# Attention and mixer on one core: rebuilt with 32-row score tiles, transposes on VectorE, packed last chunks and a list-scheduled order

## The chip, the cores and the metric

The kernel runs on 1 core of one Trainium2 chip. The metric is the device time of one execution in microseconds, given as the median of 3 runs. A core has TensorE (PE in the profile; its weight loads are PEld), VectorE (DVE), ScalarE (ACT), GpSimd (POOL) and SyncE (SP). Each engine works off its own instructions in order; DMAs are issued from the queues of POOL, SP and ACT.

## The reference

Block-wise causal attention (blocks of 64 positions), then a mixer over tokens and over channels, with both results added to what went in:

```python
B, H, S, D = 8, 8, 576, 64
scores = q @ k.T / sqrt(D)                    # per batch and head: 576 x 576
scores = where(pos_i // 64 >= pos_j // 64, scores, -1e9)
attn = softmax(scores)
x = (attn @ v) of all heads side by side      # 576 x 512 per batch
u = x + (relu(x.T @ w_tok1) @ w_tok2).T       # token mix, inner size 256
out = u + relu(u @ w_ch1) @ w_ch2             # channel mix, inner size 1536
```

All inputs and the output are fp32 in device memory; the kernel computes in bf16 with fp32 accumulation.

## The kernel before

576 rows are four chunks of 128 and a last one of 64, which is treated as a full chunk padded with zeros. The work of a batch is four `attention_pair` calls (two heads each) and one mixer.

`load_qk_pair` (lines 109 to 126) loads q and k of two heads by POOL's queue, which casts fp32 to bf16 on the way, two DMAs a head and tensor (512 rows at line 116, 64 rows at line 122). `attention_pair` (line 181) transposes q and k on PE against the identity (lines 186 and 192, five 128x128 tiles each), copies the results out of PSUM (DVE at lines 188 and 194, ACT at line 195), and so has the head dimension on the partitions: 64 rows for each of two heads. The k of one head keeps the other head's 64 rows at zero (`kTa`, `kTb`), so that a product of 128 rows gives one head's scores. Scores (line 214) are kept as keys on the partitions and queries on the columns; the table `REGIONS` cuts the causal half into six products of 512, 64, 448, 320, 192 and 64 columns, 1,600 in all. ACT takes the exponential (lines 223 to 226), DVE writes zeros into the four half blocks that the mask excludes (lines 230 to 233), and the product with v (line 238) is taken in 15 products of 65 columns, the 65th a column of ones that gives the sum. DVE takes the reciprocal (line 247) and multiplies (lines 248 and 254) into `x_sb`.

`token_mix` (line 261) is 10 products of 512 columns for `aT` (line 266) and 10 for `u_sb` (line 283), where DVE adds x (line 290). `transpose_u` turns u in 20 tiles (line 301). `channel_gT` (line 314) computes the inner layer for 576 rows as two halves of 288 columns, 12 x 2 x 4 = 96 products (line 319), each half rectified on ACT or DVE (line 326). `channel_h2_out` (line 330) takes 12 products of 512 columns for each of five chunks (line 336), DVE adds u (line 343), and SP's queue writes the batch out in two DMAs (lines 346 and 350).

The main loop (line 352) puts the mixer of the batch before between the four attention pairs of a batch. The framework sets the order on each engine from that program order. Rings of buffers limit how far ahead it runs: four raw q and k buffers, three sets of exponentials, three PSUM banks each for `sc` and `mps`, two for transposes. The first two pairs' q and k are loaded before anything else; the channel weights are issued behind the attention of batch 0 (line 385).

Of the kernel before, what the change touches and what calls it, by code (L numbers as in the profile page):

```python
# [10 lines left out]
BF16 = mybir.dt.bfloat16  # L12
EXP = mybir.ActivationFunctionType.Exp
# [5 lines left out]
class Ring:  # L19

    def __init__(self, pool, n, shape, dtype, name):
        self.tiles = [
            pool.tile(shape, dtype, name=f"{name}{i}", uniquify=False)
            for i in range(n)
        ]
        self.i = 0

    def next(self):
        t = self.tiles[self.i % len(self.tiles)]
        self.i += 1  # L30
        return t
# [3 lines left out]
def kernel(  # L35
# [11 lines left out]
    nc = tc.nc  # L47
# [5 lines left out]
    NS = (S + 127) // 128  # L53
    SCH = [min(128, S - 128 * i) for i in range(NS)]
    SP = 128 * NS
    NDM = DM // 128
    NDT = DT // 128
    NDC = DC // 128
    scale = 1.0 / math.sqrt(D)

    consts = ctx.enter_context(tc.tile_pool(name="consts", bufs=1))
    wpool = ctx.enter_context(tc.tile_pool(name="wpool", bufs=1))
    ring_p = ctx.enter_context(tc.tile_pool(name="ring_p", bufs=1))
    qkT_p = ctx.enter_context(tc.tile_pool(name="qkT", bufs=4))
    mix_p = ctx.enter_context(tc.tile_pool(name="mix_p", bufs=2))
    out_p = ctx.enter_context(tc.tile_pool(name="out_p", bufs=2))
    small_p = ctx.enter_context(tc.tile_pool(name="small_p", bufs=4))

    ps_at = ctx.enter_context(tc.tile_pool(name="ps_at", bufs=3, space=bass.MemoryType.PSUM))
    ps_tr = ctx.enter_context(tc.tile_pool(name="ps_tr", bufs=2, space=bass.MemoryType.PSUM))  # L70
    ps_mm = ctx.enter_context(tc.tile_pool(name="ps_mm", bufs=3, space=bass.MemoryType.PSUM))

    r_qraw = Ring(ring_p, 4, [128, NS, 2, D], BF16, "qraw")
    r_kraw = Ring(ring_p, 4, [128, NS, 2, D], BF16, "kraw")
    r_kta = Ring(ring_p, 4, [128, SP], BF16, "kTa")
    r_ktb = Ring(ring_p, 4, [128, SP], BF16, "kTb")
    r_v1 = Ring(ring_p, 6, [128, NS, 66], BF16, "v1")
    r_e0 = Ring(ring_p, 3, [128, 512], BF16, "e0")
    r_e1 = Ring(ring_p, 3, [128, 576], BF16, "e1")
    r_e2 = Ring(ring_p, 3, [128, 576], BF16, "e2")  # L80
    r_e3 = Ring(ring_p, 3, [128, 128], BF16, "e3")
    r_x = Ring(ring_p, 3, [128, NS, DM], BF16, "x_sb")
    r_u = Ring(ring_p, 2, [128, NS, DM], BF16, "u_sb")
    r_gt = Ring(ring_p, 2, [128, NDC, SP], BF16, "gT")

    def init_pads():
        for t in r_qraw.tiles + r_kraw.tiles:
            nc.vector.memset(t[64:128, 4], 0.0)
        for t in r_kta.tiles:
            nc.scalar.memzero(t[64:128, :])  # L90
        for t in r_ktb.tiles:
            nc.scalar.memzero(t[0:64, :])
        for t in r_v1.tiles:
            nc.scalar.memzero(t[64:128, 4, :])
            nc.vector.memset(t[:, 0:4, 64:65], 1.0)
            nc.vector.memset(t[0:64, 4, 64:65], 1.0)
        for t in r_e1.tiles + r_e2.tiles:
            nc.scalar.memzero(t[:, 512:576])
        for t in r_e3.tiles:
            nc.scalar.memzero(t)  # L100
        for t in r_x.tiles + r_u.tiles:
            nc.scalar.memzero(t[64:128, 4, :])
        for t in r_gt.tiles:
            nc.scalar.memzero(t[:, :, S:SP])

    ident = consts.tile([128, 128], BF16)
    make_identity(nc, ident)

    def load_qk_pair(b, hp, split=1):
        tiles = []  # L110
        for src, ring in ((q, r_qraw), (k, r_kraw)):
            t = ring.next()
            for hh in range(2):
                for f in range(split):
                    c0, c1 = 4 * f // split, 4 * (f + 1) // split
                    nc.gpsimd.dma_start(  # L116
                        out=t[:, c0:c1, hh, :],
                        in_=src[
                            b, 2 * hp + hh, 128 * c0 : 128 * c1, :
                        ].rearrange("(c p) d -> p c d", p=128),  # L120
                    )
                nc.gpsimd.dma_start(  # L122
                    out=t[0:64, 4, hh, :], in_=src[b, 2 * hp + hh, 512:576, :]
                )
            tiles.append(t)
        return tiles

    first_pair = load_qk_pair(0, 0)
    second_pair = load_qk_pair(0, 1)
    init_pads()  # L130

    w1_sb = wpool.tile([128, NS, DT], BF16)
    nc.gpsimd.dma_start(
        out=w1_sb[:, 0:4, :],
        in_=moe_w_tok1[0:512, :].rearrange("(c p) t -> p c t", p=128),
    )
    nc.gpsimd.dma_start(out=w1_sb[0:64, 4, :], in_=moe_w_tok1[512:576, :])
    nc.vector.memset(w1_sb[64:128, 4, :], 0.0)

    w2_sb = wpool.tile([128, NDT, SP], BF16)  # L140
    nc.gpsimd.dma_start(
        out=w2_sb[:, :, 0:S], in_=moe_w_tok2.rearrange("(c p) s -> p c s", p=128)
    )
    nc.vector.memset(w2_sb[:, :, S:SP], 0.0)

    wc1_sb = wpool.tile([128, NDM, DC], BF16)
    wc2_sb = wpool.tile([128, NDC, DM], BF16)

    def load_channel_weights():
        for c in range(NDM):  # L150
            nc.gpsimd.dma_start(
                out=wc1_sb[:, c, :], in_=moe_w_ch1[128 * c : 128 * (c + 1), :]
            )
        for c in range(0, NDC, 2):
            nc.gpsimd.dma_start(
                out=wc2_sb[:, c : c + 2, :],
                in_=moe_w_ch2[128 * c : 128 * (c + 2), :].rearrange(
                    "(c p) t -> p c t", p=128
                ),
            )  # L160

    REGIONS = {
        0: (0, 0, 0, 512),
        5: (1, 0, 512, 64),
        1: (1, 64, 128, 448),
        2: (2, 0, 256, 320),
        3: (2, 320, 384, 192),
        4: (3, 330, 512, 64),
    }

    def exp_lhsT(e, I, J):
        if J == 4:
            return e[3][:, 0:128]
        i0 = 128 * I
        if J == 0 and I == 4:
            J = 5
        tix, c0, ist, wdt = REGIONS[J]
        col = c0 + (i0 - ist)
        return e[tix][:, col : col + 128]

    def attention_pair(b, hp, x_sb, preloaded=None):
        qraw, kraw = preloaded if preloaded is not None else load_qk_pair(b, hp)

        qT_ps = ps_tr.tile([128, SP], BF16, name="trp")
        for c in range(NS):
            nc.tensor.transpose(qT_ps[:, 128 * c : 128 * (c + 1)], qraw[:, c], ident)
        qT = qkT_p.tile([128, SP], BF16, name="qT")
        nc.vector.tensor_copy(qT, qT_ps)  # L188

        kT_ps = ps_tr.tile([128, SP], BF16, name="trp")  # L190
        for c in range(NS):
            nc.tensor.transpose(kT_ps[:, 128 * c : 128 * (c + 1)], kraw[:, c], ident)  # L192
        kTh = [r_kta.next(), r_ktb.next()]
        nc.vector.tensor_copy(kTh[0][0:64, :], kT_ps[0:64, :])  # L194
        nc.scalar.copy(kTh[1][64:128, :], kT_ps[64:128, :])  # L195

        for hh in range(2):
            h = 2 * hp + hh
            kT = kTh[hh]

            v1 = r_v1.next()
            nc.gpsimd.dma_start(  # L202
                out=v1[:, 0:4, 0:64],
                in_=v[b, h, 0:512, :].rearrange("(c p) d -> p c d", p=128),
            )
            nc.gpsimd.dma_start(out=v1[0:64, 4, 0:64], in_=v[b, h, 512:576, :])  # L206

            sc_pool, sc_name = (
                (ps_mm, "mps") if (b == 0 and hh == 0) else (ps_at, "sc")
            )  # L210
            sc = [sc_pool.tile([128, 512], FP32, name=sc_name) for _ in range(4)]
            for J, (tix, c0, ist, wdt) in REGIONS.items():
                j0 = 128 * (J if J != 5 else 0)
                nc.tensor.matmul(  # L214
                    out=sc[tix][:, c0 : c0 + wdt],
                    lhsT=kT[:, j0 : j0 + 128],
                    rhs=qT[:, ist : ist + wdt],
                    start=True,
                    stop=True,
                )  # L220

            e = [r_e0.next(), r_e1.next(), r_e2.next(), r_e3.next()]
            nc.scalar.activation(e[0], sc[0], EXP, scale=scale)  # L223
# [129 lines left out]
    for b in range(B + 1):  # L353
# [15 lines left out]
        if prev is not None:  # L369
            channel_gT(p_uT, p_gT, 4, 8)  # L370
# [48 lines left out]
```

## Time and profile before

| | us |
|---|---|
| median of 3 runs | 414.12 (414.06 to 414.85) |
| span of the profiled execution | 412.9 |
| the profiled execution's time outside the span, from the median | 1.2 |
| SP's output DMA of 1 MB, issue to landing (median) | 4.3 |
| channel weight DMA of 256 KB, issue to landing (median) | 11.9 |
| HBM read / written | 35.78 MB / 9.44 MB |

The span runs from the first to the last instruction on the chip. The profile has, for each engine, the busy time and the count of its instructions; groups of instructions by line, with the mean time of one and the idle time ahead of them with what ended it; the order of time; and DMA queues with their packets. The ends of matmuls are modelled: a product's row shows its whole passage through the array, and many overlap, so the rate is read from start to start in a long run of equal products. The granted clock is given for each stretch, 1.00 being full.

### The profile page before, as it was taken

Reading aid. Unit: us, or ns where it says so; the run is one execution under the profiler, and the core shown is the slowest. Engines: PE = TensorE matmul, PEld = TensorE weight load, DVE = VectorE, ACT = ScalarE, POOL = GpSimd, SP = SyncE. Lnnn points to the kernel's source line nnn. Section 1 sums busy time; section 2 is a strip of 40 time slices with the busy share of each in tenths; the row PEclk is TensorE's granted clock in tenths of the full one; section 3 lists DMA queues with packets and bytes.
Section 4 is the critical chain, followed back from the end, with each engine's and each line's share of the span. In section 5 each row is a group of like instructions: output and inputs, shape, how many; then the busy total and the mean of one; then the engine's idle time right before and its main releaser. Section 6 shows DMA issues by size and latency. Waiting matters only on the chain.

```text
span 412.9 us, 8622 instructions
## 1 busy us (share of the span) xinstructions
PE 368.6 (89%) x3194; PEld 229.3 (56%) x3232; DVE 175.8 (43%) x674; ACT 221.4 (54%) x507; POOL 261.0 (63%) x403
## 2 busy tenths in 40 slices
PE   1676659999999999999999999999999999999996
PEld 1454247754676456744666457744666457744752
DVE  2244324543545364543554363543555363534112
ACT  9635037742677058742687058732687068730830
POOL 9999389999999775983679375973679320000000
PEclk9998859999999999999999999999999999999999
DMA  6999999999988894785668494885658550003003
GB/s 40 103 60 111 206 78 58 59 60 152 74 58 57 52 156 31 51 54 128 42 41 54 33 154 30 52 52 129 44 38 51 51 110 0 2 2 114 2 2 114
DMA packets 124730, 27.91 MB, mean 68 GB/s; under 512 B 117200, under 2 KB 119568, under 8 KB 124688
## 3 DMA queue, kind: packets, MB, share of 16 engines
q0 software_dynamic: 119824, 17.92, 60.2%
q1 hardware_dynamic: 4864, 9.44, 6.3%
q8 instruction: 26, 0.43, 0.4%
q14 instruction: 16, 0.13, 0.1%
HBM read 35.78 MB, written 9.44 MB: 110 GB/s over the span
## 4 chain that ended last, share of the span: by engine, by line
PE 52%; ACT 22%; POOL 9%; DVE 8%; DMA 5%; issue 3%; ACTq 0%; POOLq 0%
PE mps L336 22%; PE mps L319 18%; ACT e L224 6%; ACT e L223 5%; ACT kTb L195 5%; DMA wc_sb<-in_moe_w_ch_dram 4%; PE sc L238 4%; ACT e L225 3%; PE sc L214 3%; DVE u_sb L290 3%; POOL qraw L116 2%; POOL v L202 2%; ACT uT L306 2%; DVE qT L188 1%; ACT gT L326 1%
## 5 line engine op out<-in xcount | busy, mean ns | idle before, releaser
L319 PE MATMUL mps<-uT,wc_sb 128*128 128x288 bf16 x768 | 111.6, 286 | 1.0
L336 PE MATMUL mps<-wc_sb,gT 128*128 128x512 bf16 x464 | 110.8, 379 | 0.8
L319 PEld LDWEIGHTS <-wc_sb 128*128 128x128 bf16 x768 | 71.0, 97 | 28.4 <-issue 10.6
L116 POOL DMA_DIRECT2D qraw<-in_q_dram x64 | 55.3, 864 | 43.8 <-PE trp L192 28.8
L326 ACT ACTIVATE gT<-mps 128x288 bf16<-128x288 f32 x144 | 59.0, 410 | 28.1 <-PE mps L319 20.7
L336 PEld LDWEIGHTS <-gT 128*128 128x128 bf16 x480 | 44.5, 98 | 50.8 <-issue 5.1
L195 ACT COPY kTb<-trp 64x640 bf16<-64x640 bf16 x32 | 22.0, 687 | 89.5 <-DVE kTa L194 89.1
L202 POOL DMA_DIRECT2D v<-in_v_dram x64 | 56.3, 880 | 21.4 <-PE sc L214 18.5
L116 POOL DMA_DIRECT2D kraw<-in_k_dram x64 | 56.5, 883 | 7.0 <-PE trp L192 5.2
L343 DVE TENSOR_TENSOR o_sb<-mps,u_sb 128x512 f32<-128x512 f32 (+1 forms) x40 | 27.6, 690 | 71.3 <-PE mps L336 71.3
L238 PEld LDWEIGHTS <-e 128*128 128x128 bf16 x960 | 41.6, 101 | 16.9 <-issue 6.9
L214 PE MATMUL sc<-qT,kTb 128*128 128x64 bf16 (+4 forms) x190 | 43.7, 292 | 2.9 <-issue 0.4
L122 POOL DMA_DIRECT2D kraw<-in_k_dram x64 | 42.3, 660 | 1.0 <-DMA wc_sb<-in_moe_w_ch_dram 1.0
L122 POOL DMA_DIRECT2D qraw<-in_q_dram x64 | 40.9, 640 | 2.7 <-DMA wc_sb<-in_moe_w_ch_dram 2.7
L238 PE MATMUL sc<-v,e 128*128 128x65 bf16 x900 | 41.7, 195 | 1.1 <-ACT e L226 0.8
L206 POOL DMA_DIRECT2D v<-in_v_dram x64 | 41.4, 647 | 0.4 <-PE sc L214 0.3
L225 ACT ACTIVATE e<-sc 128x512 bf16<-128x512 f32 x60 | 36.0, 600 | 3.3 <-PE sc L214 1.5
L224 ACT ACTIVATE e<-sc 128x512 bf16<-128x512 f32 x60 | 35.7, 595 | 3.7 <-PE sc L214 3.7
L223 ACT ACTIVATE e<-sc 128x512 bf16<-128x512 f32 x60 | 35.8, 597 | 3.4 <-PE mps L238 1.9
L306 ACT COPY uT<-trp 128x512 bf16<-128x512 bf16 (+1 forms) x36 | 19.5, 544 | 29.9 <-PE trp L301 28.8
L326 DVE TENSOR_SCALAR gT<-mps 128x288 bf16<-128x288 f32 x48 | 22.0, 458 | 26.1 <-PE mps L319 25.6
L214 PE MATMUL sc<-qT,kTa 128*128 128x64 bf16 (+4 forms) x162 | 27.8, 280 | 4.3 <-ACT e L223 2.6
(61 smaller groups left out, 367.9 us busy)
## 6 DMA issues: line engine op xcount, KB each, us to landing
out_dram<-o_sb SPq DMA_DIRECT2D x8, 1024.0 KB, 4.3
qraw<-in_q_dram POOLq DMA_DIRECT2D x64, 64.0 KB, 2.8
kraw<-in_k_dram POOLq DMA_DIRECT2D x64, 64.0 KB, 2.7
v<-in_v_dram POOLq DMA_DIRECT2D x64, 64.0 KB, 2.8
wc_sb<-in_moe_w_ch_dram POOLq DMA_DIRECT2D x4, 384.0 KB, 6.8
wc_sb<-in_moe_w_ch_dram POOLq DMA_DIRECT2D x6, 256.0 KB, 11.9
qraw<-in_q_dram POOLq DMA_DIRECT2D x64, 8.0 KB, 2.3
kraw<-in_k_dram POOLq DMA_DIRECT2D x64, 8.0 KB, 2.3
```

The source lines that it names most:

```text
L116: nc.gpsimd.dma_start(out=t[:, c0:c1, hh, :], in_=src[b, 2 * hp + hh, 128 * c0 : 128 * c1, :].rearrange("(c p) d -> p c d", p=128),)
L122: nc.gpsimd.dma_start(out=t[0:64, 4, hh, :], in_=src[b, 2 * hp + hh, 512:576, :])
L195: nc.scalar.copy(kTh[1][64:128, :], kT_ps[64:128, :])
L202: nc.gpsimd.dma_start(out=v1[:, 0:4, 0:64], in_=v[b, h, 0:512, :].rearrange("(c p) d -> p c d", p=128),)
L214: nc.tensor.matmul(out=sc[tix][:, c0 : c0 + wdt], lhsT=kT[:, j0 : j0 + 128], rhs=qT[:, ist : ist + wdt], start=True, stop=True,)
L223: nc.scalar.activation(e[0], sc[0], EXP, scale=scale)
L224: nc.scalar.activation(e[1][:, 0:512], sc[1], EXP, scale=scale)
L225: nc.scalar.activation(e[2][:, 0:512], sc[2], EXP, scale=scale)
L238: nc.tensor.matmul(out=u_view[:, I, 0:65], lhsT=exp_lhsT(e, I, J), rhs=v1[:, J, 0:65], start=(J == 0), stop=(J == I),)
L319: nc.tensor.matmul(out=g_ps[:, 0:288], lhsT=wc1_sb[:, m, 128 * cc : 128 * (cc + 1)], rhs=uT[:, m, 288 * sh : 288 * (sh + 1)], start=(m == ...
L326: nc.any.tensor_scalar_max(gT[:, cc, 288 * sh : 288 * (sh + 1)], g_ps[:, 0:288], 0.0)
L336: nc.tensor.matmul(out=h2_ps, lhsT=gT[:, cc, 128 * si : 128 * (si + 1)], rhs=wc2_sb[:, cc, :], start=(cc == 0), stop=(cc == NDC - 1),)
```

## The change

The kernel is written anew around a list scheduler. Each step is an `Op` with one or more engines that may do it, a cost in us, its dependencies, a priority, and a PSUM pool that it takes a bank from (`take`) or gives one back to (`give`). `Plan.run` steps through a modelled time, picks for each free engine the ready operation of the lowest priority number, and returns one list; the kernel emits its instructions in that order, which nothing changes afterwards.

- Heads are taken in groups of 4. q and k of a head lie on 32 partitions (two neighbouring rows of a position pair on each), 512 bytes of source to a piece. For batch 0 they are loaded as fp32 by SP and ACT into `stage` and cast on DVE; for later batches by POOL with a cast. DVE transposes 32x32 blocks of 32-bit words (pairs of bf16), so that each head has 32 partitions with two neighbouring head dimensions side by side. Positions are permuted within blocks of 64 by this; v, `w1`, `w2` and the output are loaded or stored in the same permuted order, with DMAs of 32 partitions each (18 a batch for v, 4 for each two chunks of output).
- Scores of 4 heads: for each of the six regions, two accumulating products (even and odd head dimensions) for each of 4 heads, each on its own 32 partitions and into its own PSUM bank. `sc` is one buffer of four banks. The regions form four sets; each set waits until the exponentials of the set before are done. An exponential covers two heads (up to 1,024 columns), the last one four heads.
- The product with v stays at 15 products of 65 columns a head, in the one bank of `ups`; the multiplication behind it is one instruction of 320 columns.
- The last 64 rows of an even and an odd batch are packed into one chunk of 128 (`um_sb`, `umT`, `gmT`). The channel mix of a batch has four chunks (products of 512 columns for the inner layer), and each pair of batches has one more chunk of both.
- Attention has the lowest priority numbers (from -1000), the token mix the next (from -500), then loads and channel mix by batch.

The diff, cut to its core:

```diff
+class Plan:
...
+    def run(self):
...
+            for e in ("PE", "ACT", "DVE", "POOL", "SP"):
...
+                for o in avail:
+                    if e not in o.engines:
+                        continue
+                    if o.take and not self.free[o.take[0]]:
+                        continue
+                    if best is None or (o.prio, o.n) < (best.prio, best.n):
+                        best = o
...
+    sc = psum.tile([128, 4, 512], FP32, name="sc")
+    ups = ring(1, [128, 512], FP32, "ups", psum)
+    mm = ring(3, [128, 512], FP32, "mm", psum)
...
+    def load_heads(src, raw, b, hg, eng, dt_bytes, prio, deps):
...
+                queue.dma_start(
+                    out=raw[32 * h : 32 * h + 32].rearrange("p k r d -> p k (r d)"),
+                    in_=src[b, 4 * hg + h].rearrange("(k b r) d -> b k (r d)", b=32, r=2),
+                )
...
+    def load_qk(b, hg):
...
+            if fast:
+                st = stage[2 * hg + n]
+                eng = "ACT" if hg == 0 and n == 1 else "SP"
+                loads = load_heads(src, st, b, hg, eng, 4, prio + n, ())
...
+                loads = [P.add("DVE", dve_cost(1152, 2), emit_cast, loads + war, prio)]
+            else:
+                loads = load_heads(src, raw, b, hg, "POOL", 2, prio + n, war)
...
+                nc.vector.transpose(
+                    dst[:, 0:S, :].rearrange("p s e -> p (s e)").bitcast(I32),
+                    raw.rearrange("p k r d -> p (k r d)").bitcast(I32),
+                )
...
+    def load_v(b):
...
+                        nc.gpsimd.dma_start(
+                            out=t[p : p + 32, J, :, 0:64],
+                            in_=v[b, :, j : j + 64, :].rearrange("h (b r) d -> r b h d", r=2)[r],
+                        )
...
+    SETS = (
+        ((0, 0, 0, 512),),
+        ((0, 0, 512, 64), (64, 128, 128, 448)),
+        ((0, 256, 256, 320), (320, 384, 384, 192)),
+        ((0, 512, 512, 64),),
+    )
...
+                for c0, j0, i0, w in regions:
+                    for par in range(2):
+                        for h in range(4):
+                            r = slice(32 * h, 32 * h + 32)
+                            nc.tensor.matmul(
+                                out=sc[:, h, c0 : c0 + w],
+                                lhsT=kT[i][r, j0 : j0 + 128, par],
+                                rhs=qT[i][r, i0 : i0 + w, par],
+                                start=(par == 0),
+                                stop=(par == 1),
+                            )
...
+            op = P.add("PE", cost, emit, ready + e_war, prio + 0.1 * s, take=("sc", bank))
...
+            groups = ((0, 2), (2, 4)) if s < 3 else ((0, 4),)
...
+                    nc.scalar.activation(
+                        e[:, h0:h1, 512 * s : 512 * s + n], sc[:, h0:h1, 0:n], EXP, scale=scale
+                    )
...
+    def channel_up(b, uT_done, wc1_ready, prio):
...
+                    nc.tensor.matmul(
+                        out=mm[bank["slot"]],
+                        lhsT=wc1_sb[:, m, 128 * cc : 128 * (cc + 1)],
+                        rhs=uT[b % 2][:, m, :],
...
+    def channel_up_mixed(pair, umT_done, wc1_ready, prio):
...
+                        nc.tensor.matmul(
+                            out=mm[bank["slot"]][:, 128 * c : 128 * (c + 1)],
+                            lhsT=wc1_sb[:, m, 128 * cc : 128 * (cc + 1)],
+                            rhs=umT[pair % 2][:, m, :],
...
+    def channel_down(b, g_done, wc2_ready, u_done, prio, mixed=False):
+        chunks = [None] if mixed else list(range(4))
...
+    with tc.manual_schedule():
+        for op in P.run():
+            op.emit(op)
```

More of the change, by code (lines that the diff above doesn't have):

```diff
@@ L2 @@
+import heapq
 import math
@@ L16 @@
 MULT = mybir.AluOpType.mult
[L19 to L31, printed above, removed]
+class Op:
+    __slots__ = (
+        "engines", "cost", "deps", "emit", "prio", "take", "give", "xfer",
+        "users", "waiting", "ready", "start", "end", "engine", "n",
+    )
@@ L66 @@
[L66 to L84, printed above, removed]
@@ L106 @@
[L106 to L115, printed above, removed]
+    NDM, NDT, NDC = DM // 128, DT // 128, DC // 128
+    scale = 1.0 / math.sqrt(D)
+    assert (S, D, H, DM) == (576, 64, 8, 512)
+    NB = S // 64
@@ new lines, with ring @@
+    sb = ctx.enter_context(tc.tile_pool(name="sb", bufs=1))
+    psum = ctx.enter_context(tc.tile_pool(name="psum", bufs=1, space=bass.MemoryType.PSUM))
+    def ring(n, shape, dtype, name, pool=sb):
+        return [pool.tile(shape, dtype, name=f"{name}{i}", uniquify=False) for i in range(n)]
+    qraw = ring(3, [128, NB, 2, D], BF16, "qraw")
+    kraw = ring(3, [128, NB, 2, D], BF16, "kraw")
+    qT = ring(3, [128, S, 2], BF16, "qT")
+    kT = ring(3, [128, 640, 2], BF16, "kT")
+    v1 = ring(2, [128, 5, H, 66], BF16, "v1")
@@ new lines @@
+    e_sb = ring(2, [128, 4, 1664], BF16, "e_sb")
+    x_sb = ring(3, [128, 5, DM], BF16, "x_sb")
+    u_sb = ring(3, [128, 4, DM], BF16, "u_sb")
+    um_sb = ring(2, [128, DM], BF16, "um_sb")
+    uT = ring(2, [128, NDM, 512], BF16, "uT")
+    umT = ring(2, [128, NDM, 128], BF16, "umT")
+    aT = ring(2, [128, NDT, DM], BF16, "aT")
+    gT = ring(2, [128, NDC, 512], BF16, "gT")
+    gmT = ring(2, [128, NDC, 128], BF16, "gmT")
+    o_sb = ring(3, [128, 2, DM], FP32, "o_sb")
+    rinv = ring(4, [128, 5, 1], FP32, "rinv")
@@ L366 @@
[L366 to L388 removed]
+            if b > 0:
+                for hg in range(2):
+                    qk[b, hg] = load_qk(b, hg)
+                vv[b] = load_v(b)
```

683 lines of the change are left out of this document (432 added, 251 removed).

## The prediction

> **What bounds the kernel now.** I read the page first, then the windows of single stretches, then the order of time on PE, then the groups of one shape.
>
> ```profile
> span 412.9 us, 8622 instructions
> PE 368.6 (89%) x3194; PEld 229.3 (56%) x3232; DVE 175.8 (43%) x674; ACT 221.4 (54%) x507; POOL 261.0 (63%) x403
> ```
>
> PE is busy for 89% of the span, but that is an average over three stages. The windows (time, then busy time and count of PE, PEld, DVE, ACT and POOL, the clock, the DMA share, GB/s) separate them: the start up to the first token mix, from there to the first channel product, one whole batch in the middle, and the last batch alone.
>
> ```profile
> 0.00:41.38 41.38, 22.97 (x206) 15.23 (x209) 13.24 (x86) 25.38 (x67) 39.88 (x66) 0.96 0.91 79
> 41.38:62.90 21.52, 13.35 (x77) 7.37 (x79) 6.75 (x19) 4.86 (x9) 13.72 (x22) 0.68 1.11 138
> 182.52:228.74 46.22, 44.26 (x399) 27.63 (x404) 21.98 (x82) 26.33 (x59) 31.22 (x49) 1.00 0.68 65
> 376.71:412.90 36.19, 31.11 (x194) 18.39 (x195) 7.90 (x12) 13.03 (x30) 0.00 (x0) 1.00 0.17 58
> ```
>
> In the middle a batch takes 46.22 us at clock 1.00, with PE busy in 44.26 of them. A busy PE may still be waiting inside its pipeline, so I need the price of each product at full rate. The order of time on PE gives it: start of a run, its length, and the start of what follows.
>
> ```profile
> 156.84 3.59 PE L319 MATMUL mps<-uT,wc_sb 128*128 128x288 bf16 x28
> 160.27 0.44 PE L192 MATMUL trp<-ident,kraw 128*128 128x128 bf16 x5
> ...
> 171.85 0.63 PE L238 MATMUL sc<-v,e 128*128 128x65 bf16 x15
> 172.32 0.63 PE L214 MATMUL sc<-qT,kTb 128*128 128x320 bf16 x3
> ...
> 182.52 9.44 PE L336 MATMUL mps<-wc_sb,gT 128*128 128x512 bf16 x43
> 191.80 0.44 PE L186 MATMUL trp<-ident,qraw 128*128 128x128 bf16 x5
> ```
>
> From start to start, 28 products of 288 columns take 3.43 us (0.1225 each), 43 of 512 take 9.28 (0.2158), 15 of 65 take 0.47 (0.0313). The first two give 0.4165 ns a column and 2.5 ns a product, so 128 columns cost 0.0558 us. One batch is then 96 x 0.1225 = 11.76 (channel up) + 60 x 0.2158 = 12.95 (channel down) + 20 x 0.2158 = 4.32 (token mix) + 60 x 0.0558 = 3.35 (20 transposes of u, 40 of q and k) + 8 heads x 0.68 = 5.45 (scores, 1,600 columns in 6 products) + 120 x 0.0313 = 3.76 (exp times v) = **41.6 us**. The period is 46.2, so **4.6 us** a batch are gaps. By 62.90 PE had done the attention of batch 0 (11.4), its token mix and transposes (5.4) and one pair of batch 1 (2.9), 19.7 in all: **43 us** are lost at the start. The tail has 30.1 of work in 36.2: **6 us** lost. Check: 8 x 41.6 + 7 x 4.6 + 43 + 6 = 414, against 412.9.
>
> **The change, part by part.**
>
> *PE work.* Transposes of q and k go: -2.2 a batch. Channel up becomes 48 x 0.2158 and, for each pair of batches, 48 of 128 columns: 10.36 + 24 x 0.0558 = 11.70, nearly as before. Channel down falls from 5 chunks to 4.5: 54 x 0.2158 = 11.65, -1.3. Transposes of u are 18: 1.00. Token mix and exp times v stay, 4.32 and 3.76. Without scores: 32.4.
>
> *Scores.* For 4 heads there are 6 regions of 8 products with 32 rows, two for each head. No row of before shows a product on 32 rows. If four run side by side, a group costs 2 x 1,600 x 0.4165 ns = 1.33 us; if none do, 4 x that and 48 x 2.5 ns, 5.45. For a batch (two groups) the bounds are 2.7 and 10.9, against 5.45 now. To either I add the filling of the pipeline once a set.
>
> ```profile
> L238 PE MATMUL sc<-v,e 128*128 128x65 bf16 x900 | 41.7, 195 | 1.1 <-ACT e L226 0.8 <-DVE e L233 0.2
> L223 ACT ACTIVATE e<-sc 128x512 bf16<-128x512 f32 x60 | 35.8, 597 | 3.4 <-PE mps L238 1.9 <-PE sc L214 0.7
> L226 ACT ACTIVATE e<-sc 64x64 bf16<-64x64 f32 x60 | 12.8, 213 | 0.0
> L326 ACT ACTIVATE gT<-mps 128x288 bf16<-128x288 f32 x144 | 59.0, 410 | 28.1 <-PE mps L319 20.7
> L343 DVE TENSOR_TENSOR o_sb<-mps,u_sb 128x512 f32<-128x512 f32 x32 | 22.1, 692 | 56.2 <-PE mps L336 56.2
> L248 DVE TENSOR_TENSOR x_sb<-sc,rinv 128x256 bf16<-128x256 f32 x60 | 25.4, 424 | 1.8
> L247 DVE RECIPROCAL rinv<-sc 128x5 f32<-128x5 f32 x60 | 11.7, 195 | 19.0 <-PE sc L238 15.7
> L230 DVE MEMSET e<- 64x32 uint32 x64 | 5.4, 85 | 33.5 <-ACT e L223 31.5
> L188 DVE COPY qT<-trp 128x640 bf16<-128x640 bf16 x32 | 15.6, 486 | 24.3 <-PE trp L186 23.0 <-PE sc L214 1.3
> ```
>
> A lone product of 65 columns is modelled at 195 ns and spaced by 31: 0.165 us of filling, by 8 sets 1.3 us. I take 2.7 + 1.3 = 4.0, near the lower end, because four heads go to four banks and four sets of rows, so the products name nothing in common. A batch is then **36.4 us**, 8 of them 291 (before: 333).
>
> [...]
>
> *ACT and DVE.* ACT at 597 ns for 512 and 213 for 64 costs 158 + 0.857 a column: 1.04 us for an exp of 1,024, 0.38 for one of 256. A batch has 12 and 2: 13.2 us (before 16.0). DVE: 8 reciprocals 1.6, 8 multiplies of 320 at 0.49 = 3.9, 9.5 additions at 0.69 = 6.5, 8 memsets about 1.3 (an estimate from 85 ns for a quarter of the size), and 4 transposes of 576 words. No row shows these; the bounds are 0.2 (less than half of the 640-column copy) and 1.5 (twice an addition's), and I take 0.76, an addition's rate. DVE's own is 16. Shared between both are 15.5 rectifications at 0.6 to 0.69 and 4.5 copies: 12. Together 41 us on two engines in 38, so neither binds; even at 1.5 the transposes add 3 to DVE. What was hidden behind PE stays hidden.
>
> *The new wait.* There is one score buffer, of four banks. A set is PE 0.6, two exps 2.07, and two handovers of some 0.25 (an estimate: the 0.165 of filling and a little more): 3.2 us; a group 3 x 3.2 + 1.2 = 10.8, a batch 21.6, below 38. So the chain itself doesn't bind in the middle. But PE has one fixed order: a set that stands too early holds every product queued behind it, mixing too, and the three `mm` banks' readers with them. Exp times v has one bank, PE 0.47, two DVE operations 0.7 and handovers, about 1.6 a head, 13 a batch; also below. Gaps of 4.6 a batch are what before's order leaves. Bounds: 0.5 and that 4.6; 28 us of mixing are there to fill each batch, and I take 2.
>
> *Loads and the start.*
>
> ```profile
> L116 POOL DMA_DIRECT2D qraw<-in_q_dram x64 | 55.3, 864 | 43.8 <-PE trp L192 28.8 <-PE trp L186 11.4 <-DMA wc_sb<-in_moe_w_ch_dram 1.8
> L122 POOL DMA_DIRECT2D qraw<-in_q_dram x64 | 40.9, 640 | 2.7 <-DMA wc_sb<-in_moe_w_ch_dram 2.7
> ...
> q0 software_dynamic: 119824, 17.92, 60.2%
> q1 hardware_dynamic: 4864, 9.44, 6.3%
> ```
>
> Packets on POOL's queue take 0.602 x 412.9 x 16 / 119,824 = 33.2 ns of one engine, the 2 KB ones of SP's queue 86. Before, 13,824 packets a batch are 28.7 us of the 46. After, v keeps 4,608 (9.6 us), q and k have 4,608 of double size: 33 to 86 ns, 9.6 to 25, and I take 40 ns (nearer the smaller size), 11.5. With 3 for the output, 24 of 38 us; at the upper end 37, just short of binding. POOL issues 34 a batch at 0.64 to 0.86, 22 to 29 us. SP's output DMAs rise from 16 to 80, each on a queue with nothing else in the middle.
>
> The start is the open part. Batch 0's q and k come in fp32 by SP and ACT (11.5 us of the engines together with v's 9.6), then a cast and a transpose each: first scores at about 11 us, where before has them at 9.76.
>
> ```profile
> 9.76 1.44 PE L214 MATMUL mps<-qT,kTa 128*128 128x512 bf16 x5 [0.67 <-DVE kTa L194]
> ...
> 41.38 3.94 PE L266 MATMUL mps<-x_sb,w_sb 128*128 128x512 bf16 x10 [0.82 <-DVE x_sb L248]
> ...
> 55.23 0.69 PE L186 MATMUL trp<-ident,qraw 128*128 128x128 bf16 x5 [6.78 <-DMA qraw<-in_q_dram]
> ...
> 62.90 0.90 PE L319 MATMUL mps<-uT,wc_sb 128*128 128x288 bf16 x6
> ```
>
> Two groups in a row, 22 us, and the last heads' 6: token mix at about 40, where it begins at 41.38 now. What gets better comes behind it: by priority POOL issues v, the token weights, `wc1`, then batch 1. In engine time that is 11.5 + 9.6 + 4 + 12 x 8 x 86 ns = 8.3 + 5.8, so `wc1` and the first group of batch 1 are there at about 40, where before PE waits 6.78 us for q of batch 1 until 55.23 and channel up begins at 62.90. Then follow v of batch 1 (9.6), q (2.9), `wc2` (8.3) and k (2.9): the second group is there at 63. By 63 PE can do 7.8 + 5.3 + 11 + 3.9 = 28 us, so 35 are lost; down of batch 0 and the rest of the attention then nearly cover the wait for x of batch 1, and I add 2: **37** (bounds 28, if the loads overlap better, and 52, if 86 ns hold). The tail stays at 6: last addition, issue, landing.
>
> *Sum*: 291.4 + 7 x 2 + 37 + 6 = 348.4 in the account that gives 414 for before's 412.9 (1.2 too much); outside the span lie 414.1 - 412.9 = 1.2. Forecast **348 us** against a median of 414.12; its own range is 332 to 366.
>
> **The rivals.**
>
> [...]
> - *Everything overlaps better*: gaps 0.5, start 28: 10 + 9 less, 329. For it: ACT and DVE are idle nearly half the time. Against: x of batch 0 is late by the chain.
> - *The start stays load-bound*: 52 lost: 363. For it: the DMA share is 0.91 and 1.11 in the first two windows.
> - *The row tiles don't run side by side*, so the change doesn't do what it says: 10.9 for 2.7 a batch, 66 more: 414, or 404 without the filling. For it: operands in steps of two elements, and no row of such a product. Against: separate rows and banks.
> - *Slower: PE stands before score sets.* Each of 48 full sets can hold PE for two exps and the handovers, 2.6 us: 125 us, 473. It is slower than before from 66 / 48 = 1.4 us a set. For it: one score buffer, and an order fixed before the run. Against: 28 us of mixing a batch that can stand between sets, and 21.6 < 38.
>
> **How the numbers follow.** The forecast 0.51; emptied twice 0.15; better overlap 0.12; load-bound start 0.09; no overlap in the array 0.07; PE held by score sets 0.06. The range 324 to 380 holds the first four but for their edges, about 0.8. A measurement of this kernel can tell some 0.2% from no change. Slower gets the last case and a part of the fifth: 0.07; same 0.01; faster 0.92.
>
> **What would show it.** Right: sets of scores whose eight products of 512 columns start within some 0.45 us; no transposes of q and k on PE; a middle period of 37 to 40 us; a token mix at about 40 us and channel up right behind it; DVE transposes near 0.76 us. Wrong: score products 0.21 us apart (no overlap); PE idle put down to ACT's exps for more than 1 us a set; PE idle before scores put down to DMA far beyond 65 us; a period above 42.

## The result and the profile after

The changed kernel takes 350.57 us (median of 4 runs, 349.52 to 351.32), against 414.49 us for the kernel before beside it: a ratio of 0.8454, 95% interval 0.8436 to 0.8472. The profiled execution has a span of 348.4 us. The page of the changed kernel: its span, busy time by engine, and the row of PE in 40 slices.

```profile
span 348.4 us, 7436 instructions
PE 304.8 (87%) x2992; PEld 161.0 (46%) x3040; DVE 147.7 (42%) x353; ACT 172.3 (49%) x238; POOL 164.9 (47%) x292
...
PE   0254589996999999999999999999999999999994
```

PE's share of the span is lower than before, 87% for 89%, and yet the kernel is 15% faster: the share says nothing of how much work there was, nor where the idle time lies. The row of slices does: all of it but the tail is in the first quarter. The windows of the changed kernel (columns as above) are cut at the first token mix, near the first channel down, and at 100 us.

```profile
0.00:43.78 43.78, 15.65 (x225) 9.86 (x225) 16.95 (x48) 15.38 (x17) 35.97 (x72) 1.00 1.15 139
43.78:62.00 18.22, 16.40 (x159) 8.27 (x163) 7.94 (x19) 10.36 (x17) 11.89 (x20) 1.00 1.11 131
62.00:100.00 38.00, 33.50 (x363) 16.66 (x367) 19.00 (x44) 22.27 (x30) 35.98 (x62) 0.91 1.22 125
100.00:343.60 243.60, 239.19 (x2250) 126.19 (x2286) 103.16 (x242) 124.25 (x177) 81.11 (x140) 1.00 0.50 62
```

Busy time hides short waits (before's middle batch has PE busy for 44.26 us with 41.6 us of work), so I count each stretch's weight loads by line (PEld has no records missing: 3,040, as the code has) and price each with the rate of its product: 0.2158 us for 512 columns, 0.0558 for 128, 0.0313 for 65, and 2.26 us for the scores of a group, whose working stands in the last section but two. The groups of PEld in the last stretch of the changed kernel, 100 to 343.6 us:

```profile
L604 PEld LDWEIGHTS <-gT 128*128 128x128 bf16 x336 | 31.2, 98 | 37.1 <-issue 2.7
L538 PEld LDWEIGHTS <-wc_sb 128*128 128x128 bf16 x334 | 31.2, 98 | 37.9 <-issue 3.4
L387 PEld LDWEIGHTS <-e_sb 128*128 128x128 bf16 x660 | 25.4, 97 | 9.0 <-issue 0.5
L565 PEld LDWEIGHTS <-wc_sb 128*128 128x128 bf16 x192 | 11.1, 98 | 1.0 <-issue 0.2
L351 PEld LDWEIGHTS <-kT 32*128 32x128 bf16 x488 | 7.8, 93 | 10.2 <-issue 8.1
L504 PEld LDWEIGHTS <-u_sb 128*128 128x128 bf16 x96 | 5.8, 97 | 2.6 <-issue 2.4
L472 PEld LDWEIGHTS <-w_sb 128*128 128x128 bf16 x60 | 5.2, 98 | 6.8 <-issue 2.0
L446 PEld LDWEIGHTS <-w_sb 128*128 128x128 bf16 x54 | 4.9, 98 | 5.8 <-issue 0.6
L604 PEld LDWEIGHTS <-gmT 128*128 128x128 bf16 x48 | 4.6, 98 | 5.2
L504 PEld LDWEIGHTS <-um_sb 128*128 128x128 bf16 x12 | 0.8, 97 | 0.6 <-issue 0.4
L446 PEld LDWEIGHTS <-w1o_sb 128*128 128x128 bf16 x6 | 0.6, 98 | 0.7
```

That is 838 x 0.2158 + 300 x 0.0558 + 660 x 0.0313 + 488/768 x 36.2 = 241.2 us of work in 243.6. At the left edge loads run ahead of their products, by some 0.3 us of work (the loads at 99.82 and 99.88 are of products that stream until 100.31); with that, PE loses **2 us** from 100 us on. The same count for both kernels, in us of the profiled executions:

| | before | forecast | after |
|---|---|---|---|
| PE's work, 8 batches | 332.7 | 291.4 | 295.6 |
| lost at the start | 43.7 (to 62.9) | 37 | 45.9 (to 100) |
| lost in the middle | 30.2 | 14 | 2.1 |
| lost at the end | 6.3 | 6 | 4.8 |

So 37 of the 64 us came from less work and 27 from time that PE no longer loses (80.2 before, 52.8 after). The start has next to no part in it: the two columns end it at different times, and by the same count the kernel before had lost 46 us at 100 us too.

Lost time is counted against PE's full rate, and not all of it is waiting. In the first 47 us PE runs at about half that rate: the set of 512 columns at 22.93 takes 0.97 us from start to start, where a set takes 0.56 later.

```profile
22.93 1.04 PE L351 MATMUL sc<-qT,kT 32*128 32x512 bf16 x8
23.90 1.00 PE L387 MATMUL ups<-v,e_sb 128*128 128x65 bf16 x15
```

The clock column has 1.00 there, against these rows. In the run with k first (below) column and rows agree; here are two stretches of its start and a set in each:

```profile
25.10:28.48 3.38, 0.64 (x16) 0.27 (x16) 1.60 (x6) 2.64 (x4) 3.08 (x6) 1.00 1.13 176
28.50:48.90 20.40, 13.36 (x148) 7.71 (x149) 6.61 (x20) 7.00 (x9) 19.07 (x33) 0.50 1.19 124
```

```profile
26.08 0.64 PE L351 MATMUL sc<-qT,kT 32*128 32x64 bf16 x16 [1.10 <-ACT e_sb L366]
...
31.64 1.04 PE L351 MATMUL sc<-qT,kT 32*128 32x320 bf16 x16
```

An estimate from such rows: six full sets 0.41 us longer and the last four products with v 0.38 longer each make some 4 us of the first 43.78. In the changed kernel the clock is at half once more, in the hole of PE between 82 and 92 us:

```profile
84.84:91.67 6.83, 5.01 (x40) 2.21 (x34) 2.60 (x7) 2.81 (x4) 5.93 (x10) 0.50 1.32 182
```

No run changed the clock by itself, so what it costs was not measured.

### The profile page after: what moved, and what is told of

It reads as the page before. It is cut to its first block, busy times and chain, and to the rows that moved or that the text cites. A ratio compares the mean times of both kernels' runs of the same rounds, so it can differ in the third digit from the quotient of the medians.

```text
span 348.4 us, 7436 instructions
## 1 busy us (share of the span) xinstructions
PE 304.8 (87%) x2992; PEld 161.0 (46%) x3040; DVE 147.7 (42%) x353; ACT 172.3 (49%) x238; POOL 164.9 (47%) x292
## 3 DMA queue, kind: packets, MB, share of 16 engines
q1 hardware_dynamic: 9536, 11.21, 13.4%
## 4 chain that ended last, share of the span: by engine, by line
PE 62%; POOL 16%; DMA 13%; issue 4%; DVE 4%; ACT 0%; POOLq 0%; DVEq 0%
PE mm L538 21%; PE mm L604 20%; POOL v L262 7%; PE ups L387 5%; PE sc L351 5%; DMA wc_sb<-in_moe_w_ch_dram 5%; PE mm L446 4%; DMA v<-in_v_dram 4%; PE mm L472 3%; POOL qraw L215 3%; PE mm L565 3%; POOL kraw L215 3%; DMA kraw<-in_k_dram 2%; PE mm L504 2%; DVE u_sb L485 1%
## 5 line engine op out<-in xcount | busy, mean ns | idle before, releaser
L366 ACT ACTIVATE e_sb<-sc 128x1024 bf16<-128x1024 f32 (+1 forms) x112 | 99.3, 932 | 72.3 <-PE sc L351 70.7
L538 PE MATMUL mm<-uT,wc_sb 128*128 128x512 bf16 x369 | 87.4, 379 | 1.5 <-issue 1.0
L604 PE MATMUL mm<-wc_sb,gT 128*128 128x512 bf16 x368 | 85.7, 379 | 1.4 <-issue 1.0
L427 ACT ACTIVATE gT<-mm 128x512 bf16<-128x512 f32 x86 | 51.4, 597 | 71.6 <-PE mm L538 71.6
L351 PE MATMUL sc<-qT,kT 32*128 32x64 bf16 (+4 forms) x768 | 37.6, 301 | 24.3 <-DVE qT L242 12.3
L538 PEld LDWEIGHTS <-wc_sb 128*128 128x128 bf16 x384 | 35.8, 98 | 43.0 <-issue 3.8
L387 PEld LDWEIGHTS <-e_sb 128*128 128x128 bf16 x960 | 39.7, 102 | 20.3 <-issue 10.1
L387 PE MATMUL ups<-v,e_sb 128*128 128x65 bf16 x960 | 43.4, 200 | 5.9 <-DVE x_sb L408 5.8
L215 POOL DMA_DIRECT2D qraw<-in_q_dram x56 | 34.1, 637 | 7.6 <-DMA wc_sb<-in_moe_w_ch_dram 5.9
L215 POOL DMA_DIRECT2D kraw<-in_k_dram x56 | 34.0, 632 | 2.7 <-DMA kraw<-in_k_dram 1.5
L373 DVE MEMSET e_sb<- 64x128 uint32 x64 | 10.2, 165 | 13.4 <-ACT e_sb L366 10.0
```

Source lines behind the costliest of these rows:

```text
L215: queue.dma_start(out=raw[32 * h : 32 * h + 32].rearrange("p k r d -> p k (r d)"), in_=src[b, 4 * hg + h].rearrange("(k b r) d -> b k (r d ...
L351: nc.tensor.matmul(out=sc[:, h, c0 : c0 + w], lhsT=kT[i][r, j0 : j0 + 128, par], rhs=qT[i][r, i0 : i0 + w, par], start=(par == 0), stop=(p ...
L366: nc.scalar.activation(e[:, h0:h1, 512 * s : 512 * s + n], sc[:, h0:h1, 0:n], EXP, scale=scale)
L387: nc.tensor.matmul(out=u[:, I, 0:65], lhsT=e[:, h, c : c + 128], rhs=vt[:, J, head, 0:65], start=(J == 0), stop=(J == I),)
L427: nc.scalar.activation(dst, src, RELU)
L538: nc.tensor.matmul(out=mm[bank["slot"]], lhsT=wc1_sb[:, m, 128 * cc : 128 * (cc + 1)], rhs=uT[b % 2][:, m, :], start=(m == 0), stop=(m == ...
```

## The experiments

Theory 1 was that PE's work sets the time wherever PE isn't starved, and that the 32-row products of four heads run side by side; the rivals were slack on PE, the order, and the loads at the start. All ratios are against the kernel before, measured beside the runs.

**Row tiles.** The two loops in a region are swapped:

```diff
-                    for par in range(2):
-                        for h in range(4):
+                    for h in range(4):
+                        for par in range(2):
```

> The loops inside a score region are swapped: the two products of a head (even and odd head dimensions, on the same 32 rows) follow each other, and then the next head's. Nothing else changes, the fixed order of all steps included. Theory 1 (products on different rows run side by side, on the same rows they don't, and PE's work sets the time): a region is then a staircase of 5 widths where it was 2, so a group of 4 heads costs 3 x 1,600 x 0.4165 ns = 2.0 us more, 16 groups 32 us: about 382 us, and the eight products of a 512-column region span some 1.1 us instead of 0.43. Rival 1 (the products never overlapped, and the time was saved elsewhere): no change, 350. Rival 2 (they overlap, but PE has slack that takes up the extra work): 350 to 362.

Measured: 351.11 us, 0.847 (0.8455 to 0.8484): no change. Taken alone that would fit rival 1, but the rows of the order of time on PE contradict it. Four score products are under way in the 0.05 us from 170.47 on, and the wider window has all eight:

```profile
170.46 0.41 PE L351 MATMUL sc<-qT,kT 32*128 32x512 bf16 x4
...
170.46 0.64 PE L351 MATMUL sc<-qT,kT 32*128 32x512 bf16 x8
171.03 1.25 PE L472 MATMUL mm<-aT,w_sb 128*128 128x512 bf16 x5
```

Eight products of 512 columns, 1.7 us if taken one by one (8 x 0.2158), leave PE after 0.57 us. In the changed kernel, where the first products of all four heads stand ahead of the second ones, four start at 170.48 and the other four at about 170.72: two products on the same rows start 0.24 us apart there. In this run the two of a head stand together, and four products are under way in the first 0.06 us all the same. So I take it that products of other heads, on other rows, went ahead of the second one. (The rows don't name the head, so this is inferred from the program's order.) By that, what the first section says of engines, that each works off its instructions in order, doesn't hold for PE's products on different rows. So both theories were wrong in one part: the products do run side by side, and they need not stand side by side in the program (351.11 us for 350.57). The staircase that I expected assumed that a product waits for all that stand ahead of it.

**Packing.** Each batch gets a mixed chunk of its own, with half its rows in use (core of the edit):

```diff
-        pair = b // 2
+        pair = b
...
-            if p % 2 == 1:
-                gm_done = channel_up_mixed(p // 2, um_done, wc1_ready, 10 * p + 3.5)
+            if True:
+                gm_done = channel_up_mixed(p, um_done, wc1_ready, 10 * p + 3.5)
```

> Every batch gets a last chunk of its own, half filled, as before the change: 4 more of the packed chunks. By the rates of the trace each costs 48 x 0.0558 + 12 x 0.2158 + 4 x 0.0558 = 5.5 us of PE. Theory 1 (PE's work sets the time from about 100 us on): 22 us more, 372. Rival 2 (PE has slack, the order or the loads set the time): well below, 352 to 360. If the additional PSUM evacuations and banks bind as well: above 376.

Measured: 365.14 us, 0.8812 (0.8788 to 0.8837): 14.6 us more, not 22. By the same count PE has 317.6 us of work, 22.0 more, as worked out; what is lost between 62 and 100 us falls from 7.4 to 2.0. The added chunk of batch 0 fills the hole at the start. Of the 22.0 us, 14.6 came through to the time and 5.4 went into that hole; the other 2.0 are less lost elsewhere (45.4 lost in all, for 52.8).

**Order.** Attention is kept one batch ahead of the mixer, behind older channel work:

```diff
-        prio = -1000 + 10 * b + 4 * hg
+        prio = 10 * (b - 1) + 0.2 * hg
```

> The priority of attention is set so that it runs one batch ahead of the mixer, behind older channel work, as in the order of before; all instructions stay. Theory 1 in its plain form (there is enough mixing work to fill PE whichever way the steps are ordered): 350 to 356. Rival 3 (the gaps of 4.6 us a batch went because attention runs ahead and is always first; with one batch ahead the chain of one score buffer and one bank for exp times v shows again): 7 x 4 = 28 us more, about 378.

Measured: 357.32 us, 0.8612 (0.8599 to 0.8625): 6.7 more, just outside the plain theory's range and far from the rival's. By the count the start is as it was (46.1 lost), and from 100 us on 9.2 us are lost for 2.0. Running ahead is worth about 7 us. PE loses 60.0 us of this run's span in all, against 80.2 before and 52.8 in the changed kernel, so 20 of the 27 us stay without it; what part of these the list's order has and what the new steps have wasn't separated.

**Loads.** The last channel weights go behind k of batch 1's second head group on POOL's queue:

```diff
-            done2.append(P.add("POOL", 0.66, emit, (), 15.0, xfer=32 * 0.098))
+            done2.append(P.add("POOL", 0.66, emit, (), 15.5, xfer=32 * 0.098))
```

> On POOL's queue the last channel weights (3 DMAs of 512 KB) are moved behind k of the second head group of batch 1, which now waits for them until 63.8 us. Theory 4 (the PE idle time between 82 and 98 us comes from x of batch 1, late through that k): 3 to 6 us less, 345 to 347. Rival 4 (the start is bound by the sum of the loads, their order is of no account): 350 within 1 us. If the channel weights become late for channel down instead: 351 to 355.

Measured: 344.92 us, 0.8315 (0.8302 to 0.8327): 5.7 less, as theory 4 has it. The changed kernel's DVE rows in the order of time show what was late, and the window from 62 to 100 us with k first, against 33.50 above, what closed:

```profile
63.83 0.78 DVE L242 STREAM_TRANSPOSE kT<-kraw 128x576 int32<-128x576 int32 x1 [3.07 <-DMA kraw<-in_k_dram]
```

```profile
62.00:100.00 38.00, 37.20 (x411) 19.12 (x416) 23.10 (x54) 23.28 (x32) 35.85 (x62) 1.00 1.15 109
```

To see whether the loads as a whole hold the start, the channel weights were left out, first with the old order and then with an order made for it:

```diff
-                    nc.gpsimd.dma_start(
-                        out=wc1_sb[:, m, 512 * f : 512 * f + 512],
-                        in_=moe_w_ch1[128 * m : 128 * (m + 1), 512 * f : 512 * f + 512],
-                    )
+                    nc.gpsimd.memset(wc1_sb[:, m, 512 * f : 512 * f + 512], 0.01)
...
-            done2.append(P.add("POOL", 0.66, emit, (), 15.0, xfer=32 * 0.098))
+            done2.append(P.add("POOL", 0.66, emit, (), 15.0))
```

(`wc2` in the same way; the second part, with the `xfer` of `wc1` too, only in the second run.)

> The 15 DMAs of the two channel weights are left out; POOL writes a constant into those tiles in their place, so the output is not the reference's. Theory 4 (the start is bound by the loads: POOL's queue and the 16 engines are never free in the first 80 us): q, k and v of batch 1 come some 10 to 16 us earlier: 336 to 342. Rival 6 (the start is bound by the chain of scores, exponentials, product with v and multiplication of batch 0, which begins at 12.3 us and ends at 43.8 with one buffer of each): at most what moving k gave, 344 to 348.

> The channel weights are left out once more and replaced by a constant that POOL writes (the output is not the reference's), but the scheduler is told that nothing is transferred, so the fixed order is made anew for the early arrival of batch 1. In the run with the old order PE's steps stood at the same times as with the loads. Theory 7 (order counts: a load that arrives early gains only where the order uses it; the first 43 us are the chain of batch 0): the hole between 62 and 100 us closes as with k first, the first 43 us stay: 343 to 346. Theory 4 (loads bind the start as a whole): the first 43 us shrink too: 335 to 341. If the order is of no account: 349 as with the old order.

Measured: 349.45 us, 0.8416 (0.8382 to 0.8449), with the old order; 344.40, 0.8293 (0.8278 to 0.8308), with the new one. Neither theory of the first run held: with 6.3 MB fewer to read it is hardly faster, because the order of every engine was fixed for a k that comes at 64 us, and PE's windows stay as they were, with 33.60 us busy between 62 and 100:

```profile
62.00:100.00 38.00, 33.60 (x361) 16.48 (x365) 17.38 (x42) 22.21 (x30) 37.10 (x65) 0.91 1.18 117
```

With the order remade the hole closes, and the result is that of k first, with all loads in place. Its first 43.5 us still lose 33.9, for 34.6 in the changed kernel: theory 7. So the channel loads as a sum don't bind the start; their order did, and what is left is the chain of batch 0. That chain begins with a wait for batch 0's own q and k (first scores at 12.3 us), which none of the runs shortened.

**The chain of batch 0.** The copies of the second token weights were put behind the last multiplication of batch 0 on DVE (their `deps` become `[ld, x_done[0][-1]]`), with k first:

> The k of batch 1 stands ahead of the last channel weights as in the run above, and the four copies of the second token weights on DVE are put behind the last multiplication of batch 0. In the changed kernel they stand ahead of a reciprocal of batch 0 on DVE, wait there for their load until 26.8 us, and hold two products with v and through them a score set by about 2.3 us. Rival 6 (the chain of batch 0 sets the start once k is early): 2 us less than with k alone, 343. Theory 4 in its plain form (loads alone): the same as with k alone, 345 within 0.7 us.

Measured: 343.78 us, 0.8298 (0.8268 to 0.8329), 1.1 less than k first, within the intervals: not told apart from it. Then two more steps, alone and together:

```diff
+        ub, upool = (mm, "mm") if b == 0 else (ups, "ups")
...
-            av = P.add("PE", mm_cost(65, 15) + 0.08, emit, exps + v_ready + x_war, prio + 1, take=("ups", bank))
+            av = P.add("PE", mm_cost(65, 15) + 0.08, emit, exps + v_ready + x_war, prio + 1, take=(upool, bank))
```

> K first and the w2 copies late, and besides the product with v of batch 0 takes its PSUM banks from the three of the mixer, which has nothing to do then, in place of the single one. Theory 6 (the single bank makes each head wait for the multiplication of the head before, 0.8 to 2.2 us of PE each between 28.8 and 43.4 us): the first token mix 3 to 4 us earlier, 340 to 341. Rival (the heads wait for exponentials anyway): 343 to 344.

Measured: 342.81 us, 0.8253 (0.8237 to 0.8270): faster than the changed kernel and than k first by their intervals, the best of all by its median, but only 1 us less than the run before it, where 3 to 4 were expected, and not told apart from that by its interval. The rows of PE in that run show why:

```profile
30.96 1.04 PE L351 MATMUL sc<-qT,kT 32*128 32x320 bf16 x16 [2.04 <-ACT e_sb L366]
34.04 0.30 PE L351 MATMUL sc<-qT,kT 32*128 32x64 bf16 x8 [2.04 <-ACT e_sb L366]
...
39.22 0.98 PE L388 MATMUL mm<-v,e_sb 128*128 128x65 bf16 x15 [2.30 <-DVE x_sb L409]
```

The sets still come 3.1 us apart, each waiting 2.04 us for the exponentials of the one before: the single score buffer sets the pace until 34 us. Behind it three of the last heads now follow each other without a wait, 45 products from 34.27 on, but the fourth waits until 39.22. Its bank comes free late because DVE, in its fixed order, stands at a transpose of batch 1's q ahead of the multiplications of batch 0, and that q is still under way:

```profile
37.78 0.78 DVE L242 STREAM_TRANSPOSE qT<-qraw 128x576 int32<-128x576 int32 x1 [3.40 <-DMA qraw<-in_q_dram]
```

So the first token mix comes at 42.23, where the run before has 42.00. What the banks gain is lost again to a load and its place in the order; the runs don't show what theory 6 is worth without that.

```diff
-    qk[0, 1] = load_qk(0, 1)
+    qk[0, 1] = load_qk(0, 1, qk[0, 0])
```

(the third argument becomes the loads' `deps`)

> K first and the w2 copies late, and besides q and k of batch 0's second head group are issued only once the first group's are transposed, so the first group has the DMA engines to itself but for v. Theory 8 (the first 12.3 us are the shared DMA engines): first scores 2 to 3 us earlier, 341 to 342. Rival 8 (the first group's time is latency and issue; the second group then becomes late instead): 343 to 346.

> All four: k first, w2 copies late, second group later, three banks for batch 0. If theories 6 and 8 hold and add up: 337 to 339. If the first 43 us are one chain, in which what one gains the other waits for: 340 to 342.

Measured: 347.25 us, 0.8371 (0.8354 to 0.8389), and 344.43, 0.8299 (0.8278 to 0.8320). Theory 8 was not tested by this. A dependency given to the scheduler only sorts the list, and SP's queue had nothing else to send in between: the loads left when they did before, within 0.4 us. The changed kernel's row of the issues into `stage` (first and last start), and then that run's:

```profile
L215 SPq DMA_DIRECT2D stage<-in_k_dram x4: 312/382/455, 7.9 to 9.4; - x4
```

```profile
L215 SPq DMA_DIRECT2D stage<-in_k_dram x4: 312/382/456, 8.1 to 9.8; - x4
```

What did change was the order on DVE, made for a late load, and that cost 3.5 us against the run without the step: a multiplication of batch 0 now stands behind the same transpose of batch 1's q, and PE waits 4.24 us for it until 39.30, for 2.39 without the step. Whether the shared DMA engines make the first scores late (12.3 us) stays open.

**Changes of shape.** One product of 65 columns on 128 rows inside each set (`if par == 1 and c0 == 0`), and in the companion the same product behind each set:

```diff
+                            nc.tensor.matmul(
+                                out=ups[0][:, 400:465], lhsT=ident, rhs=ident[:, 0:65],
+                                start=True, stop=True,
+                            )
```

> In each of the 64 score sets one product of 65 columns on all 128 rows (identity by identity, into 65 unused columns of the bank of exp times v) is put between the even and the odd products of the first region, so that the array leaves the 32-row products and comes back once more a set. The fixed order of all other steps is the same. Theory 5 (each change between 32-row and 128-row products empties the array: the trace of the changed kernel has some 0.1 us beyond the streaming time on either side of a set): 64 x (0.03 + 0.2) = 15 us of PE, of which some of the first 16 sets' share is hidden in the start: 361 to 366. Rival 5 (those 0.1 us are handovers between engines or the filling of any product, not the change of shape): as in the companion run with the product behind the set, 350 to 354.

> The companion: the same 64 products of 65 columns on 128 rows, but directly behind each score set, where the array changes to 128 rows anyway. Theory 5: 64 x 0.03 = 2 us of PE and no change of shape more: 350.5 to 353. If an additional product as such costs its whole passage of 0.2 us: 362.

Measured: 367.20 us, 0.885 (0.8829 to 0.8871), inside; 357.85, 0.8618 (0.8569 to 0.8666), behind. The order of time on PE, a set of 512 columns with what follows it, first with the product inside, then behind:

```profile
182.16 0.41 PE L356 MATMUL sc<-qT,kT 32*128 32x512 bf16 x4
182.49 0.20 PE L350 MATMUL ups<-ident 128*128 128x65 bf16 x1
182.63 0.40 PE L356 MATMUL sc<-qT,kT 32*128 32x512 bf16 x4
182.97 0.39 PE L477 MATMUL mm<-aT,w_sb 128*128 128x512 bf16 x1
```

```profile
177.23 0.63 PE L351 MATMUL sc<-qT,kT 32*128 32x512 bf16 x8
177.79 0.20 PE L363 MATMUL ups<-ident 128*128 128x65 bf16 x1
177.83 0.38 PE L481 MATMUL mm<-aT,w_sb 128*128 128x512 bf16 x1
```

From the set's start to the next step it is 0.81 us with the product inside and 0.60 with it behind, which itself adds 0.04 to the 0.56 of the changed kernel. One more pair of changes costs **0.21 us**, for the 0.2 that theory 5 put in; that the array empties at a change is its reading, which no row shows by itself. The times of the runs lie outside both ranges of theory 5, 367.20 for 361 to 366 and 357.85 for 350.5 to 353. By runs the difference is 9.4 us where 64 x 0.21 = 13.4 are worked out; some of that lies in the start. The companion is 4 us slower than its 2.6 us of work accounts for, and its runs scatter from 355.08 to 359.27. The added products write into the bank of exp times v and wait for its readers (1.8 us in the waits); the rest I can't place.

## Why the forecast held, step by step

The forecast was 348 us and the measured time is 350.57, but three of its terms were off and cancel; that the sum came so near is luck.

- *PE work* was right but for the scores: 295.6 us for 291.4. The rows of the changed kernel, exp times v with a channel product behind it and with a set behind it:

```profile
157.89 0.61 PE L387 MATMUL ups<-v,e_sb 128*128 128x65 bf16 x15
158.34 1.89 PE L538 MATMUL mm<-uT,wc_sb 128*128 128x512 bf16 x8
...
169.93 0.62 PE L387 MATMUL ups<-v,e_sb 128*128 128x65 bf16 x15
170.48 0.63 PE L351 MATMUL sc<-qT,kT 32*128 32x512 bf16 x8
171.04 1.25 PE L472 MATMUL mm<-aT,w_sb 128*128 128x512 bf16 x5
```

  The set takes 0.56 us where two widths stream in 0.43 by the rate per column, and the 15 products ahead of it take 0.55 where they take 0.45 otherwise. So a set costs 0.10 + 0.13 beyond streaming, not the 0.165 that I put in once; a full set is 0.66, the last (0.18, and 0.10) 0.28, a group 2.26 for my 2.0. No run shows the case "emptied twice", which has 0.15 among the chances, as a time of its own; what the rows show is this 0.23 a set, and 0.21 for one more pair of changes of shape.
- *Gaps in the middle* were taken as 2 us a batch and are 2 us in all from 100 us on. My reason, mixing work enough to fill, was right where attention runs ahead (one batch ahead it was 9.2); half of before's loss was too cautious. The part of the rival "everything overlaps better" that speaks of gaps came true.
- *The start* is the step that failed: 37 forecast, 45.9 measured. The load times were right (the second group of batch 1 expected at 63, its k is transposed at 63.83). By 63 us 38.5 are lost for 35. Token mix comes at 43.78 for "about 40": first scores at 12.30 for 11, and the last four heads take 8.9 us, from 34.85 on, for 6, with a score set of batch 1 among them that waits 1.05 us for its k and takes 0.97. The two groups between take 22.5 us for 22, but by luck: a set costs 0.97 us for 0.6 at half rate, and the two handovers 0.17 for 0.5. The forecast priced this chain at full rate, though its own windows of the start have the clock at 0.96 and 0.68. The larger part is behind it. Wrong was that channel down of batch 0 and the rest of attention would "nearly cover the wait for x of batch 1", for which I added 2 us: the hole is 7.4, with the stretch at half clock in it, and the moved channel weights close nearly all of it.
- *The durations on ACT and DVE* came out as worked out:

```profile
L366 ACT ACTIVATE e_sb<-sc 128x1024 bf16<-128x1024 f32 x96 | 93.2, 1024 | 63.4 <-PE sc L351 61.8 <-issue 1.2
...
L408 DVE TENSOR_TENSOR x_sb<-ups,rinv 128x320 bf16<-128x320 f32 x64 | 31.2, 487 | 1.6
...
L242 DVE STREAM_TRANSPOSE qT<-qraw 128x576 int32<-128x576 int32 x16 | 12.4, 777 | 8.8 <-PE sc L351 6.2 <-DMA qraw<-in_q_dram 2.5
```

  1.02 us for 1.04, 0.49 for 0.49, and 0.777 for the transposes that no row of before showed, where I took 0.76.
- *The rivals.* No overlap in the array, and PE standing before score sets, are refuted: the waits of the changed kernel (in all, times, longest) have 10.5 us of PE waiting for exponentials, and by the order of time five of the seven, 9.3 us, lie in the first 35 us, where there is no mixing work to put between. The start bound by loads is refuted as a sum of the channel loads and right as an order.

```profile
PE sc L351 <- ACT e_sb L366: 10.5, 7, 2.0
```

## What to carry to other kernels

Account for PE by counts and rates, stretch by stretch: a forecast can be right as a sum while its terms err by 9 and 12 us, and only the account shows where the next gain lies. Take the rate of each stretch from its rows: a start at half rate can stand under a clock column that says 1.00. Where the order is fixed before the run, look at what an early load can reach: here it gained 1.1 us, within the intervals, under the old order and 6.2 with the order made anew. A dependency that only the planner knew of held no load back here (8.1 to 9.8 us for 7.9 to 9.4). When a rewrite has made the middle dense, look at the start: there three DMAs moved behind four others were worth more than everything else tried.

## What the runs showed of the hardware that was not expected

As far as the program's order tells which product is which, products on different groups of 32 rows did not wait for one another in program order: with both products of a head adjacent, four products were under way within 0.06 us, where two on the same rows start 0.24 us apart in the changed kernel, and a set took 0.57 us as against 0.56 with the heads inside. One more pair of changes between 32-row and 128-row products cost 0.21 us, some half of the 0.43 us that eight products of 512 columns need to stream. PE ran at about half rate for the first 47 us of the changed kernel (0.97 us from start to start for a full set, 0.56 later), and its granted clock fell to 0.50 for 6.83 us from 84.84 on; with k first, where PE has no hole there, the clock from 62 to 100 us reads 1.00.
